# Retention and a maxout FFN on one core: key scaling moved from GpSimd to ScalarE, and the order of retention's VectorE steps changed

## The chip, the cores and the metric

One core of a Trainium2 chip runs the whole program. The metric is the device time of one execution in microseconds (us). Five runs of the kernel before took 780.17 to 783.39 us, median 781.77. All data is fp32.

## The reference, cut to what matters

```python
# B, H, S, D = 8, 8, 576, 64;  4608 tokens, d_model 512 = H*D, d_ff 768
scores = q @ k.T / sqrt(D)                       # per batch and head
ret    = scores * gamma[h] ** (i - j)  (0 where j > i)
x      = (ret @ v).transpose(0, 2, 1, 3).reshape(4608, 512)
h      = max(x @ w1, x @ w2, x @ w3)             # 4608 x 768
out    = h @ w_out                               # 4608 x 512
```

The decay gamma^(i-j) is split into a factor for the query's row and one for the key's row. So keys are multiplied by a factor per row and head (the table `gk`, 128 rows x 8 heads), and the result by a query's factor (`gq`). The weights arrive as 64-bit floats and are turned into fp32 on the chip.

## The kernel before, in words

**Two parts that run together.** The tokens are cut into 36 chunks of 128 (`g`), four to a tile of 512 tokens (`t`, 0 to 8). For each tile `ffn(t)` (L681) does the FFN, and while it runs, retention of tile t+1 is done between its matmuls. `ffn` is a generator that stops 12 times a tile; at stop m the main loop (L831) issues what `steps(t + 1)` (L795) has put into slot m. So a slot is a twelfth of a tile.

**The FFN.** The 768 columns are six groups `fb` of 128. Tile 0 multiplies plainly, while VectorE and ScalarE still convert weights (`convert`); tile 1 does groups 2 and 3 plainly, then 0, 1, 4, 5 by products; tiles 2 to 8 do 0, 1, 4, 5, 2, 3, all by products. "By products" is a scheme with fewer multiplications (`up`, L619): 20 block products a group in the order of `PRODUCTS` (L66), each written to PSUM as A, B, C, D or E. A and B share two PSUM buffers, and C, D and E two others. ScalarE copies each finished A and B to SBUF (L633); VectorE adds and compares them in 14 joins a group (L628), which also read C, D and E from PSUM and so free their buffers. Then `downs` (L467) multiplies by `w_out` in seven products with the tags `dx`, `dy`, `dz`; sums of h (L465) and sums of its outputs are made by VectorE and GpSimd.

**Retention of a chunk, from tile 1 on.** Its keys (`kraw`, 128x512) and values are loaded by SP's DMAs; `load` is itself put into the queue `urgent`. `decay(g)` (L230) scales the keys in place on GpSimd, in one instruction (L236). `transposes(g)` (L244) makes transposed keys and queries: on TensorE with copies on ScalarE for chunks 4 to 6, by two VectorE transposes from chunk 7 on. `chunk_scores(g)` (L287) does the matmuls of scores and state (`sk`, L294 and L298), and then four VectorE steps: two masks (`mask`, L302), which turn `sk` into masked scores `m`, and two `keep_chunk` steps (L310), which carry the state `va` on; after the second one GpSimd multiplies the state by `gs_of` (L312). `values(a, b)` (L354) does the output matmuls `o` (L378) of a pair of chunks, and `output` the multiplication by `gq` and, at a tile's end, 13 sums of x (`X_SUMS`).

**What sets VectorE's order.** The order on each engine is that in which the program issues. From tile 1 on, retention's VectorE steps don't go out at once: `soon` (L177) appends them to the queue `urgent`. During a group of products, `ffn` lets one out after every odd step and every fifth step, 12 of 20. `scores()` and `values()` begin by letting out all that is still there (`chore(len(urgent))`). So the four steps of a pair's first chunk all go out as soon as the second chunk's `scores` starts; those of the second chunk go out one by one. Sums of weights stand in a second queue, `chores`.

**Slots of a pair (a, b), before.** m: transposes(b), decay(b). m+2: scores(a), scores(b), load of b+2. m+3: decay(a+2). m+4: values(a, b), transposes(a+2), load of a+4. Here m is 0 for a tile's first pair and 6 for its second. Chunks 4 to 7, during tile 0, have an order of their own.

**Buffers.** Raw keys have three buffers, raw queries and transposable keys two, state `va` four, PSUM tiles for retention four (`ps_r`).

**The start.** Chunks 0 to 3 are done before `ffn(0)`, in the order written at L751 to L793: loads, decay, transposes, scores, state and values of each. `key_masks` (L343, GpSimd) makes the mask table `gm`; `carry` (L337, ScalarE) copies the last state and the factors `gs_of`.

Of the kernel before, what the change touches and what calls it, by code (L numbers as in the profile page):

```python
# [45 lines left out]
ALU = mybir.AluOpType  # L46
# [34 lines left out]
def kernel(  # L81
# [14 lines left out]
    nc = tc.nc  # L96
    P = 128
    B, H, S, D = q.shape
# [6 lines left out]
    CPT = NT // C  # L105
# [21 lines left out]
    gk = const.tile([C, H], FP32, name="gk")  # L127
# [24 lines left out]
    raws, vds, vas, qks, ms, sts, states, kvs = {}, {}, {}, {}, {}, {}, {}, {}  # L152
# [10 lines left out]
    def half(j):  # L163
        return slice(D * j, D * (j + 1))

    def place(g, c):

        return (g * C + D * c) % S // D

    late, chores, urgent, spread = {}, deque(), deque(), []  # L170

    def chore(n=1):
        for _ in range(n):
            if urgent or chores:
                (urgent or chores).popleft()()
# [54 lines left out]
    def decay(g):  # L230
        factor = gk[:].unsqueeze(2).to_broadcast([C, H, D])
        if g < CPT:
            t = vds[g] = vpool.tile([C, H, D], FP32, tag="va1", name="vd")
            nc.gpsimd.tensor_tensor(t[:], raws.pop(("v", g))[:], factor, op=ALU.mult)
            return
        nc.gpsimd.tensor_tensor(raws["k", g][:], raws["k", g][:], factor, op=ALU.mult)  # L236
        for c in range(2):
            if place(g, c) == 0:
                nc.gpsimd.memset(vas[g, c][half(1 - c)], 0.0)
# [28 lines left out]

    def scores(g):
        chore(len(urgent))  # L270
        if g >= CPT:
            chunk_scores(g)
            return
        qT, kT = qks[g]["q"], qks[g]["k"]
        s = [ps_r.tile([C, NP, C], FP32, tag="r", name=f"s{j}") for j in range(2)]
        for p in range(NP):
            for j in range(2):
                r = half(j)
                nc.tensor.matmul(s[j][:, p, :], lhsT=kT[r, p, :], rhs=qT[r, p, :], start=True, stop=True)
        for j in range(2):  # L280
            t = sts[g, j] = att.tile([C, NP, C], FP32, tag=f"m{j}", name="st", bufs=3)
            nc.vector.tensor_tensor(t[:], s[j][:], causal[:].unsqueeze(1).to_broadcast([C, NP, C]), op=ALU.mult)
# [54 lines left out]
    def carry():  # L337

        for j in range(2):
            nc.scalar.copy(vas[CPT, 0][half(1), j::2, :], states[CPT][half(j)])  # L340
            nc.scalar.copy(gs_of[half(1), j::2].unsqueeze(2), gs[half(j), :, 0:1])

    def key_masks():  # L343
        for c in range(2):
            nc.gpsimd.tensor_tensor(gm[half(c)], causal[half(c), half(c)].unsqueeze(1).to_broadcast([D, H, D]),
                                    gk[half(c)].unsqueeze(2).to_broadcast([D, H, D]), op=ALU.mult)
# [252 lines left out]
    def weight_sums(fp):  # L599

        def step(dst, a, sign, b):
            combine(*(factor(n, slice(2 * fp, 2 * fp + 2)) for n in (dst, a, b)), sign)

        for dst, _, a, sign, b in W_SUMS:
            chores.append(partial(step, dst, a, sign, b))
        chores.append(partial(summed_fp.add, fp))

    def late_room():
        pool = late["pool"]
        late["W"] = [pool.tile([P, NF, P], FP32, name=f"n{n}") for n in range(1, 9)]  # L610
        late["X"] = {n: pool.tile([P, NH], FP32, name=n)[:] for n in sorted({x[0] for x in X_SUMS})}
# [3 lines left out]
    def convert(n):  # L615
        for _ in range(n):
            next(converting, None)
# [60 lines left out]
    def ffn(t):  # L678

        h = hpool.tile([P, NF, NT], FP32, tag="h", name="h")  # L680
        if t == 0:  # L681
            for fp, i in units:
                for fb in (2 * fp, 2 * fp + 1):
                    maximum = up_plain(t, h, fb, i)
                    if CPT not in qks:
                        maximum()
                        transposes(CPT)
                        decay(CPT)
                        convert(4)
                        continue  # L690
                    convert(4)
                    maximum()
                yield
            convert(6)
            for fb, _ in enumerate(downs_plain(t, h)):
                convert(4 if fb < 2 else 4 * len(pieces))
                if fb == 2:
                    while_converting.close()
                    late["pool"] = ctx.enter_context(tc.tile_pool(name="late", bufs=1))
                    late_room()  # L700
                    sums_of_outs()
                elif fb > 2:
                    chore({3: 4, 4: 0, 5: 2}[fb])
                if fb in (1, 3):
                    yield
            yield
            return
        if t == 1:
            spread.append(True)
            weight_sums(0)  # L710
            weight_sums(2)
        plain = (2, 3) if t == 1 else ()
        order = (2, 3, 0, 1, 4, 5) if t == 1 else (0, 1, 4, 5, 2, 3)
        total = sum(24 if fb in plain else len(PRODUCTS) for fb in order)
        count = parts = 0
        for n, fb in enumerate(order):
            if fb not in plain:
                while fb // 2 not in summed_fp:
                    chore()
            steps_of_one = up_plain_all(t, h, fb) if fb in plain else up(t, h, fb)  # L720
            for step, cost in enumerate(steps_of_one):
                if fb in plain:
                    chore(4 if (fb, step) == (plain[-1], 1) else 8)
                elif step % 2 or step % 5 == 4:
                    chore(len(urgent) > 0)
                elif step % 4 == 2 and chores:
                    chores.popleft()()
                count += cost or 1
                if count * (NF // 2 * 3) >= (parts + 1) * total:
                    parts += 1  # L730
                    yield
            if n % 2:
                sums_of_hidden(h, fb // 2)
                if fb in plain:
                    weight_sums(fb // 2)
        chore(len(urgent))
        for n, _ in enumerate(downs(t, h)):
            chore(4)
            if n in (1, 3):
                yield  # L740
        yield
# [13 lines left out]
    load_weights(1)  # L755
    load(CPT)
    decay(0)
    transposes(0)
    for c in range(2):
        of_rows = out_decay[:, NP // 2 * c:NP // 2 * (c + 1), :].rearrange("(b p) u c -> p b (u c)", b=2)  # L760
# [8 lines left out]
    scores(1)  # L769
    first_output()  # L770
    transposes(2)
    decay(2)
    load_values(CPT)
    load_weights(4)
    state(1)
    keep(1)
    values(1)
    transposes(3)
    decay(3)
    scores(2)  # L780
    scores(3)
    state(2)
    keep(2)
# [4 lines left out]
    convert(4)  # L788
    state(3)
    keep(3)  # L790
    key_masks()
    carry()
    convert(2)  # L793

    def steps(t):  # L795


        todo = [[] for _ in range(3 * CPT)]

        def at(n, *what):  # L800
            for step, *args in what:
                args = [g for g in args if g < NG] if step is values else args
                if args and args[0] < NG:
                    todo[n].append(partial(soon, partial(step, *args)) if step is load else partial(step, *args))

        if t == 1:
            a, b, c, d = range(CPT, 2 * CPT)
            at(0, (load, b))
            at(1, (scores, a))
            at(2, (transposes, b), (decay, b), (load, c))  # L810
            at(3, (scores, b), (load_blocks, d, 0))
            at(4, (load_blocks, d, 1, 2))
            at(5, (values, a, b), (load_blocks, d, 3), (load, d))
            at(6, (transposes, c), (decay, c), (load_blocks, d + 1, 0))
            at(7, (transposes, d), (decay, d), (load_blocks, d + 1, 1, 2))
            at(8, (scores, c), (scores, d), (load_blocks, d + 1, 3), (load, d + 1))
            at(9, (load_blocks, d + 2, 0, 1))
            at(10, (decay, d + 1), (load_blocks, d + 2, 2))
            at(11, (values, c, d), (load_blocks, d + 2, 3), (load, d + 2), (transposes, d + 1))
            return todo  # L820
        for n in range(0, CPT, 2):
            a, b, m = CPT * t + n, CPT * t + n + 1, 6 * (n // 2)
            at(m, (transposes, b), (decay, b))
            if a == 2 * CPT:
                at(m, (load, a + 2))
            at(m + 2, (scores, a), (scores, b), (load, b + 2))
            at(m + 3, (decay, a + 2))
            at(m + 4, (values, a, b), (transposes, a + 2), (load, a + 4))
        return todo

    for t in range(N // NT):  # L831
# [56 lines left out]
```

## Time and profile before

| | before |
|---|---|
| five runs | 781.13, 781.77, 783.39, 781.93, 780.17 us, median 781.77 |
| the profiled execution's own time | 781.13 us |
| its span in the profile | 779.4 us |
| mean granted TensorE clock | 0.991 |
| GpSimd, key scaling, 128x512 (L236) | 32 instructions, 1.13 us each |
| GpSimd, state times `gs_of` (L312) | 28 instructions, 1.177 us each |
| ScalarE, copies of A and B (L633) | 276 and 230 instructions, 0.372 us each |
| VectorE, mask of half a chunk (L302) | 64 instructions, 0.688 us each |
| DMA, mean | 76 GB/s |

How to read it: the span runs from the first to the last instruction, and the execution's own time is 1.7 us longer. Busy times are of one engine each and overlap. PE is TensorE's matmuls, PEld its weight loads, DVE is VectorE, ACT ScalarE, POOL GpSimd, SP the engine that issues DMAs. In a line of the timeline the first two numbers are start and length, a name `out<-in` gives the buffers, a shape partitions x elements, xN counts instructions drawn together, and a bracket names the wait in front and what ended it. Engines run their own queues in order, so an instruction that waits holds up all behind it on that engine.

### The profile page before, as it was taken

The page shows a single profiled execution, that of the slowest core. Times are in us where ns is not written, and L with a number is a line of the kernel's source. Part 1 is how long each engine was busy: PE and PEld are TensorE (multiplying, and loading weights), DVE is VectorE, ACT ScalarE, POOL GpSimd, SP SyncE. Part 2 cuts the span into 40 slices and gives each one's busy share as a digit, 9 for nine tenths or more (in the row PEclk, how much of TensorE's full clock was granted, in tenths as well). Part 3 has the DMA queues.
Part 4 walks back from the last instruction along what each step waited for, and adds up shares of the span by engine and source line. Part 5 has one row for each costly group of instructions (what it writes and reads, how often), then busy time and mean ns, then how long its engine had stood idle before and what let it go on. Part 6 is the DMA issues. An engine that isn't in the chain of part 4 may idle for free.

```text
span 779.4 us, 16192 instructions
## 1 busy us (share of the span) xinstructions
PE 751.0 (96%) x6040; PEld 607.5 (78%) x6040; DVE 615.1 (79%) x1270; ACT 353.6 (45%) x869; POOL 125.0 (16%) x138
## 2 busy tenths in 40 slices
PE   8799989999899999999989999999989998999998
PEld 7544444488788888888878887888878887888887
DVE  2889999799979876988598959886889678865672
ACT  3676642155145524462345435451546064524651
POOL 2310113031203030203030302110122003010000
PEclk9989999999999999999999999999999999999999
DMA  9986751424042413342243325141515141001001
GB/s 226 229 203 144 200 116 55 84 52 84 14 105 45 78 46 83 68 77 47 68 83 56 58 66 95 29 82 59 90 28 98 40 88 37 1 15 41 1 1 54
DMA packets 230110, 59.40 MB, mean 76 GB/s; under 512 B 210960, under 2 KB 228752, under 8 KB 230032
## 3 DMA queue, kind: packets, MB, share of 16 engines
q1 hardware_dynamic: 229456, 58.04, 34.4%
q8 instruction: 47, 0.77, 0.4%
q10 hardware_dynamic: 576, 0.33, 0.2%
q14 instruction: 31, 0.25, 0.1%
HBM read 48.89 MB, written 9.44 MB: 75 GB/s over the span
## 4 chain that ended last, share of the span: by engine, by line
PE 74%; DVE 17%; ACT 3%; issue 2%; DMA 2%; SPq 1%; POOL 0%; DVEq 0%; ACTq 0%
PE a L648 15%; PE b L648 13%; PE dx L488 10%; PE c L648 7%; PE dz L488 5%; DVE part L628 5%; PE e L648 5%; PE d L648 4%; PE o L378 4%; PE down L658 3%; DVE m L302 3%; PE up L671 3%; DVE va L310 2%; PE dy L488 2%; PE sk L294 2%
## 5 line engine op out<-in xcount | busy, mean ns | idle before, releaser
L628 DVE TENSOR_TENSOR part<-part 128x256 f32<-128x256 f32 x460 | 221.9, 492 | 64.1 <-ACT part L633 56.2
L633 ACT COPY part<-a 128x256 f32<-128x256 f32 x276 | 102.8, 372 | 73.3 <-PE a L648 60.4
L633 ACT COPY part<-b 128x256 f32<-128x256 f32 x230 | 85.7, 372 | 101.7 <-PE b L648 93.0
L671 PE MATMUL up<-xT,w 128*128 128x512 f32 (+2 forms) x200 | 87.0, 590 | 3.2 <-DVE w L577 3.2
L312 POOL TENSOR_TENSOR va<-va,gs_of 64x512 f32<-64x512 f32 x28 | 33.0, 1177 | 325.9 <-DVE va L310 165.7
L648 PE MATMUL a<-s,w 128*128 128x256 f32 x276 | 82.7, 381 | 0.7 <-ACT part L633 0.7
L648 PE MATMUL b<-s,n 128*128 128x256 f32 x276 | 82.2, 379 | 0.2 <-ACT part L633 0.2
L671 PEld LDWEIGHTS up<-xT,w 128*128 128x128 f32 x200 | 37.5, 194 | 46.6 <-issue 39.7
L648 PE MATMUL d<-s,w 128*128 128x256 f32 x184 | 55.6, 384 | 8.4 <-DVE part L628 8.4
L648 PEld LDWEIGHTS a<-s,w 128*128 128x128 f32 x276 | 51.9, 190 | 9.2 <-ACT part L633 1.9
L648 PEld LDWEIGHTS b<-s,n 128*128 128x128 f32 x276 | 52.4, 190 | 7.7 <-ACT part L633 0.7
L648 PE MATMUL c<-xT,w 128*128 128x256 f32 x184 | 56.0, 386 | 0.0
L648 PE MATMUL b<-xT,n 128*128 128x256 f32 x184 | 55.3, 382 | 0.0
L302 DVE TENSOR_TENSOR m<-sk,gm 64x512 f32<-64x512 f32 x64 | 44.1, 688 | 5.1 <-PE sk L298 4.0
L628 DVE TENSOR_TENSOR h<-part 128x256 f32<-128x256 f32 x92 | 42.7, 464 | 6.9
L648 PE MATMUL e<-xT,w 128*128 128x256 f32 x184 | 47.2, 379 | 0.0
L648 PE MATMUL a<-xT,n 128*128 128x256 f32 x184 | 47.2, 379 | 0.0
L648 PEld LDWEIGHTS d<-s,w 128*128 128x128 f32 x184 | 34.7, 191 | 14.6 <-DVE part L628 10.0
L488 PE MATMUL dx<-To,H 128*128 128x256 f32 (+1 forms) x204 | 44.9, 370 | 0.0
L495 ACT COPY part<-dx 128x256 f32<-128x256 f32 (+1 forms) x34 | 10.5, 362 | 74.1 <-PE dx L488 74.1
L465 POOL TENSOR_TENSOR H<-h,H 128x256 f32<-128x256 f32 x24 | 19.2, 801 | 152.5 <-DVE H L464 128.9
L633 ACT COPY part<-d 128x256 f32<-128x256 f32 x92 | 34.3, 372 | 15.3 <-PE d L648 10.2
(119 smaller groups left out, 1383.6 us busy)
## 6 DMA issues: line engine op xcount, KB each, us to landing
bits<-in_moe_w_dram SPq DMA_DIRECT2D x36, 256.0 KB, 4.6
out_dram<-osb SPq DMA_DIRECT2D x35, 256.0 KB, 2.1
kraw<-in_k_dram SPq DMA_DIRECT2D x32, 256.0 KB, 3.0
va<-in_v_dram SPq DMA_DIRECT2D x64, 128.0 KB, 3.2
qraw<-in_q_dram SPq DMA_DIRECT2D x232, 32.0 KB, 2.2
kxraw<-in_k_dram SPq DMA_DIRECT2D x232, 32.0 KB, 2.1
bits<-in_moe_w_out_dram SPq DMA_DIRECT2D x6, 512.0 KB, 3.9
qraw<-in_q_dram SPq DMA_DIRECT2D x6, 256.0 KB, 4.3
```

Of the source, the lines that this page charges most:

```text
L294: nc.tensor.matmul(sk[c][half(c), h, :], lhsT=kr[half(c), h, :], rhs=vas[g, c][half(c), h, :], start=True, stop=True)
L302: nc.vector.tensor_tensor(ms[g, c][half(c)], sk[1 - c][half(c)], gm[half(c)], op=ALU.mult)
L310: nc.vector.tensor_tensor(to[half(c)], sk[c][half(c)], vas[g, c][half(1 - c)], op=ALU.add)
L312: nc.gpsimd.tensor_tensor(to[half(1)], to[half(1)], gs_of[half(1)].unsqueeze(2).to_broadcast([D, H, D]), op=ALU.mult)
L378: nc.tensor.matmul(o[0][half(c), n % 2, n // 2, half(m)], lhsT=vas[g, m][:, h, :], rhs=ms[g, m][:, h, :], start=m == 0 and n == 0, stop=Tr ...
L465: urgent.append(lambda: (pool(s3, a11, a21, op=ALU.subtract), pool(s4, a12, s2, op=ALU.subtract)))
L488: nc.tensor.matmul(o, lhsT=hS[n](fp)[:, m * P:(m + 1) * P], rhs=late["T"][n][:, fp, cols], start=first and fp == 0 and (m == 0 or last and ...
L628: nc.vector.tensor_tensor(out, a, b, op=op)
L633: nc.scalar.copy(t[:], ps[step[0]][:])
L648: nc.tensor.matmul(ps[chain][:], lhsT=factor(w, fb), rhs=xS[t][x], start=n == 1, stop=ends, skip_group_check=True)
L658: nc.tensor.matmul(b[:], lhsT=h[:, fb, m * P:(m + 1) * P], rhs=w_sb["out", fb], start=(fb == 0), stop=(fb == NF - 1))
L671: nc.tensor.matmul(ps[:, cols], lhsT=w_sb[i, fb][:, dc * P:(dc + 1) * P], rhs=xT[t][:, dc, cols], start=dc == 0 and cols.start == 0, stop= ...
```

## The change

1. **Keys to ScalarE.** From tile 1 on, `decay` no longer issues one GpSimd multiplication of 128x512 but puts eight ScalarE multiplications of 128x64 (one head each, with the head's column of `gk` as a factor per partition) into a new queue, `scaling`. One goes out at every third step of a group of products (`step % 3 == 2`), two after each product of `downs`, and what is left at the start of `scores`. It concerns chunks 10 to 35: GpSimd has 26 fewer instructions and ScalarE 208 more.
2. **A thinner queue.** `urgent` is let out after steps with `step % 4 == 1`, five of 20, and after other odd steps only if more than six are waiting. Tile 1 keeps the rate of before.
3. **One slot earlier.** Scores of a pair go out at m+1 instead of m+2, the scaling of a+2 at m+2, that of b+2 at m+3 (it was at the start of the next pair, m+6). Values stay at m+4. The first pair of tile 2 is the exception: its scores stay at m+2, its values go to m+5.
4. **The first chunks.** `key_masks` goes from behind all chunks to just after `decay(0)`. `carry` goes into `ffn(0)`, after `decay(4)`, and its two copies of `gs_of` become `state_factors`, after `transposes(2)`. `scores(2)` goes ahead of `transposes(3)`.

Instructions per engine: TensorE and SP have the same ones in the same number, VectorE the same ones in another order.

```diff
+    late, chores, urgent, scaling, spread = {}, deque(), deque(), deque(), []
+
+    def scale(n=1):
+        for _ in range(min(n, len(scaling))):
+            scaling.popleft()()
...
-        nc.gpsimd.tensor_tensor(raws["k", g][:], raws["k", g][:], factor, op=ALU.mult)
+        kr = raws["k", g]
+        if spread:
+            scaling.extend(partial(nc.scalar.mul, kr[:, h, :], kr[:, h, :], gk[:, h:h + 1]) for h in range(H))
+        else:
+            nc.gpsimd.tensor_tensor(kr[:], kr[:], factor, op=ALU.mult)
...
     def scores(g):
         chore(len(urgent))
+        scale(len(scaling))
...
-            nc.scalar.copy(gs_of[half(1), j::2].unsqueeze(2), gs[half(j), :, 0:1])
+    def state_factors():
+        for j in range(2):
             nc.scalar.copy(gs_of[half(1), j::2].unsqueeze(2), gs[half(j), :, 0:1])
...
                         decay(CPT)
+                        carry()
...
-                elif step % 2 or step % 5 == 4:
+                elif step % 2 and (step % 4 == 1 or t == 1 or len(urgent) > 6) or t == 1 and step % 5 == 4:
                     chore(len(urgent) > 0)
...
+                if step % 3 == 2:
+                    scale()
...
             chore(4)
+            scale(2)
...
     decay(0)
+    key_masks()
     transposes(0)
...
     transposes(2)
+    state_factors()
     decay(2)
...
     values(1)
+    scores(2)
     transposes(3)
     decay(3)
-    scores(2)
     scores(3)
...
-    key_masks()
-    carry()
...
-            at(m, (transposes, b), (decay, b))
-            if a == 2 * CPT:
-                at(m, (load, a + 2))
-            at(m + 2, (scores, a), (scores, b), (load, b + 2))
-            at(m + 3, (decay, a + 2))
-            at(m + 4, (values, a, b), (transposes, a + 2), (load, a + 4))
+            first_pair = a == 2 * CPT
+            s = m + 2 if first_pair else m + 1
+            at(m, (transposes, b))
+            if first_pair:
+                at(m, (decay, b), (load, a + 2))
+            at(s, (scores, a), (scores, b), (load, b + 2))
+            at(s + 1, (decay, a + 2))
+            at(s + 2, (decay, b + 2))
+            at(s + 3, (values, a, b), (transposes, a + 2), (load, a + 4))
```

## The prediction

> **What bounds the kernel now.** I read the page first, then who waited for whom, then the stretch of time around the longest wait on each engine. From the page:
>
> ```profile
> PE 751.0 (96%) x6040; PEld 607.5 (78%) x6040; DVE 615.1 (79%) x1270; ACT 353.6 (45%) x869; POOL 125.0 (16%) x138
> ...
> PE   8799989999899999999989999999989998999998
> DVE  2889999799979876988598959886889678865672
> ...
> PEclk9989999999999999999999999999999999999999
> ```
>
> TensorE is busy nearly always, so a gain can come only from places where it stands still or its clock is low. Work per tile is fixed: 20 products a group, each two records 0.216 apart (0.432 us). Starts of TensorE records that came later than this pace add up to little, and the view of waits names their cause:
>
> ```profile
> PE d L648 <- DVE part L628: 8.4, 4, 2.3
> PE dy L488 <- DVE h L628: 3.8, 3, 2.4
> ...
> PE sk L298 <- ACT m L263: 2.4, 1, 2.4
> ```
>
> (Columns: total us, times, longest.) The four waits of `d` lie at 406, 487, 569 and 651 us, once a tile in tiles 4 to 7. Here is the first one on TensorE, VectorE and GpSimd (start, length):
>
> ```profile
> 403.34 0.59 PE L648 MATMUL a<-s,n 128*128 128x256 f32 x2
> 406.22 0.70 PE L648 MATMUL d<-s,w 128*128 128x256 f32 x2 [2.29 <-DVE part L628]
> ```
>
> ```profile
> 391.61 1.39 DVE L302 TENSOR_TENSOR m<-sk,gm 64x512 f32<-64x512 f32 x2 [0.34 <-PE sk L298]
> 393.01 1.41 DVE L310 TENSOR_TENSOR va<-sk,va 64x512 f32<-64x512 f32 x2
> 394.46 0.68 DVE L302 TENSOR_TENSOR m<-sk,gm 64x512 f32<-64x512 f32 x1
> 395.07 1.00 DVE L628 TENSOR_TENSOR part<-part 128x256 f32<-128x256 f32 x1
> ...
> 399.18 2.79 DVE L628 TENSOR_TENSOR part<-part 128x256 f32<-128x256 f32 x3
> 402.01 1.12 DVE L628 TENSOR_TENSOR h<-part 128x256 f32<-128x256 f32 x1
> ...
> 405.74 0.42 DVE L628 TENSOR_TENSOR part<-e,part 128x256 f32<-128x256 f32 x1
> ```
>
> ```profile
> 399.29 1.22 POOL L312 TENSOR_TENSOR va<-va,gs_of 64x512 f32<-64x512 f32 x1 [3.50 <-PE e L648]
> 400.59 1.10 POOL L236 TENSOR_TENSOR kraw<-kraw,gk 128x512 f32<-128x512 f32 x1
> ...
> 402.12 0.72 POOL L465 TENSOR_TENSOR H<-h 128x256 f32<-128x256 f32 x1
> ```
>
> Product 13 (`d`) takes the PSUM buffer of `e`, so it needs the join of E and B1 (`part<-e,part`). That join stands in VectorE's queue behind eight retention steps (masks L302, keeps L310, 0.69 each) and 13 joins. VectorE has no gap from 391.61 to 406.16: 14.55 us. TensorE, meanwhile, wants 12.2: of the scores' 2.1 us (390.33 to 392.44) 0.8 is left at 391.61, then products 7 to 19 and 0 to 12, 26 x 0.432 = 11.2, and 0.2 of small gaps. The difference, 2.35, is the stall (2.45 over the pace). Second reading: a join of two SBUF tiles takes 422 ns alone (376 of the 460 `part<-part`), and 807 on average when a GpSimd step overlaps it. In the 14.55 us this adds 0.58 + (2.79 - 1.35) + 0.70 = 2.7 us, of which one L236 is about 0.72 (1147 against 422).
>
> Over the pace, tiles 2 to 7 lose 1.59, 0.87, 2.45, 2.73, 2.56 and 3.95 us: 14.15 in all. The last has 1.1 us of half clock behind its stall (64 `o` records take 3.10 instead of 2.02). Tile 1 loses 2.59 at 201.67 (`dy` waits for h). Tile 8, which has no retention to do, loses nothing.
>
> **The change, part by part.**
>
> *Keys to ScalarE.* GpSimd loses 26 of its 32 L236 (1.13 each; chunks 10 to 35), ScalarE gains 26 x 8 = 208 pieces of 128x64. No row shows such a piece. ScalarE bounds: a 64x4 copy out of SBUF takes 0.19, and the nearest form with a per-partition operand is
>
> ```profile
> L561 ACT ACTIVATE expo<-expo,inf 128x512 int32<-128x512 f32 x24 | 17.3, 722 | 0.8
> ```
>
> Copies of 256 and 512 columns (372, 579 ns) give 0.81 ns a column, so 722 - 448 x 0.81 = 0.36 us; I take it, by this row's form. 208 x 0.36 = 75 us on an engine with 426 us free. What counts is the queue: a piece stands between the copy of a B and of an A, and TensorE's next A waits for the latter. The cover:
>
> ```profile
> 382.67 0.37 ACT L633 COPY part<-b 128x256 f32<-128x256 f32 x1 [0.49 <-PE b L648]
> ...
> 383.33 0.59 PE L648 MATMUL b<-s,n 128*128 128x256 f32 x2
> ```
>
> The copy ends at 383.04, 0.29 before the next `b`; TensorE resumes 0.06 after its releaser (406.16 to 406.22), so a copy may be 0.23 late. Queued ScalarE steps start 0.09 before the former ends (two L290 of 0.61 take 1.14). A copy, then the piece, then the A copy: 0.28 + 0.27 = 0.55 after the B copy's start instead of 0.43: 0.12 late, hidden. From 0.47 us a piece on, the cover is gone. At 0.72 each of some 91 pieces (136 lie in the products, four of six at such a spot) costs 0.25: 22 us. The first piece also waits for its keys' DMA, with all copies behind it: the keys of chunk a+2 are issued at 388.45 and 389.09 and land 3 us later, 392.1; the copy before the piece is at 393.6, so 1.5 us is spare. SP's order is unchanged; later transposes delay its later transfers by some 4 us, and those keys then have 3 us left.
>
> The Trainium skill speaks against this: "VectorE: DVE Perf Modes", The TRN2 errata, says that each SBUF-source instruction of VectorE and ScalarE pays its fixed latency anew, and advises tiles of 512 elements or more; "ScalarE: Activation LUTs", What ACT_TABLE_LOAD costs, would make a piece 186 + 93 + 53 = 0.33 us by estimate, so eight cost 2.7 us for one 1.13. The trace makes both harmless while ScalarE idles over half the time; by that price the copy is 0.09 late instead of 0.12.
>
> *Retention's steps spread, scores one place (1/12 tile) earlier.* The four steps of chunk a still go at once, those of b at every fourth product. Counted in the new order, from the first mask to the end of the next E join VectorE has 6 retention steps (4.15), 10 joins (4.25) and one L312 overlap (0.58): 9.0 us. TensorE has 0.8 + 6 + 13 products (8.2) + 0.2 = 9.2. So the stall goes; for 0.5 us of error either way I keep 0 to 0.5 and take 0.2 per half tile. What is late next: the `dy` behind the second half: 9.0 + two keeps, eight joins, one overlap (5.5) = 14.5 against 9.2 + 7 products + `dx` + two `dy` (6.5) = 15.7; it holds by 1.2. Tiles 2 to 7: 14.15 - 12 x 0.2 = 11.7 gained. The GpSimd part alone would leave 2.35 - 0.72 = 1.6 a tile.
>
> *Tile 1* keeps its faster rate; its eight steps move from the fourth group before the third one's end. By its rows they start at 183.66, and 8 x 0.69 + 11 joins (4.7) + a weight sum (0.4) + 0.72 end the next E join at 195.0. TensorE would have been there at 180.6 + 2.2 + 8 x 0.432 + 5.6 = 191.9: a new stall of 3.1. Then 7 products, `dx` and two `dy` lead to 201.5, where it is 201.67 now: no gain, bounds -1 to +1.
>
> *First chunks.* Today ScalarE waits 2.7 us for the state (30.97) before `carry`, and the copies of the first chunks stand behind that; `sk` starts at 37.31, 3.4 us after `up` ended, and the clock then stands at 0.52 until 43.7. After: the carry comes last, the mask tables (2.4 us of GpSimd) leave the place where they stretch three conversions by 0.84, and 31.0 is when the h copy starts; eight copies (3.0) bring `sk` to about 35.0. But up to 108 us VectorE's weight conversion sets the end (TensorE waits for w at 66 and w_out at 108), so only VectorE's lead counts: the conversion that waits for `mant` at 38.34 gets it at 31.4 + 0.6 + 3.0 + 0.75 (carry) + 0.75 = 36.5: 1.8 gained. Bounds 0 (given back at a DMA) and 4 (the clock dip after 108.4 goes too). Scores(2) ahead of the transposes: 0.3, inside this.
>
> **Sum:** 11.7 + 1.8 + 0 = 13.5; 781.13 (profiled execution; span 779.4) less 13.5 is 767.6. The median of the runs, 781.77, lies 0.64 above: **768**.
>
> **Rivals.** *The burst stays too long* (chance 0.20): if a spread step costs VectorE more or a GpSimd overlap falls on one more join (0.72), the stall returns at the E join in both halves: 0.2 + 0.7 each, 12 x 0.7 = 8.4 less: 776. For it: the margin is 0.2 us. Against: L236 leaves just this stretch. *No measurable change* (0.05): the edit only moves stalls, as in tile 1. *ScalarE's queue becomes the bound* (0.13): slower from about 0.61 us a piece on (91 x 0.14 = 13), with 0.72: 781.1 - 13.5 + 22 = 790. For it: the only ScalarE rows with a pointer operand are 0.72 to 0.76. Against: those have eight times the columns. Forecast itself (within 763 to 772): 0.62.
>
> What a measurement can tell from no change is about 0.2% (1.6 us). Faster 0.62 + 0.20 = 0.82, same 0.05, slower 0.13. The range 763 to 777 holds forecast and first rival, with the tile 1 and head bounds in it.
>
> **What would show it.** Right: `d` and `dy` waits for VectorE at 406 to 651 gone or under 0.5, tile period near 78.5 instead of 81.6; a new `d` wait of about 3 in tile 1; `sk` near 35; pieces of 0.3 to 0.4 us; no `a` wait for ScalarE. Wrong: `PE a` waiting for ScalarE often; pieces over 0.47; a ScalarE wait for `kraw`'s DMA; the E join still late in tiles 4 to 7.

## The result, and the profile after

The changed kernel takes 779.83 us (median of 32 runs, 775.83 to 781.54) where the kernel before takes 781.77: a ratio of 0.9969, 95% interval 0.9960 to 0.9978. It is faster, by 0.3% where 1.8% were forecast. The profiled execution took 778.52 us (before: 781.13).

First the page of the changed kernel: busy time, then the slices and the clock.

```profile
PE 752.0 (97%) x6040; PEld 603.7 (78%) x6040; DVE 595.8 (77%) x1270; ACT 396.7 (51%) x1077; POOL 93.4 (12%) x112
...
PE   8898989998999999999999999999999999999998
...
PEclk9999999999899999999999999999999999999999
...
L174 ACT ACTIVATE kraw<-kraw,gk 128x64 f32<-128x64 f32 x208 | 66.9, 349 | 0.3
```

GpSimd lost 32 us, VectorE 19 without losing an instruction, and a key piece takes 0.349 us. TensorE's busy time *rose* by 1.0 at equal work, and one slice near 200 us has a lower clock. The last row holds the key pieces; ScalarE waited only 0.3 us in front of all 208 of them.

Who waited for whom on TensorE in tiles 2 to 7 (220 to 704 us; total us, times, longest; a third row, 0.5 us of `sk`, is left out):

```profile
PE a L660 <- ACT part L645: 2.9, 4, 1.4
PE d L660 <- DVE part L640: 2.1, 8, 0.6
```

The four `d` waits of up to 2.3 us are gone, as forecast; eight small ones of 0.6 at most are left. What has grown is `a` waiting for ScalarE. In these tiles of the kernel before it was:

```profile
PE a L648 <- ACT part L633: 0.7, 3, 0.3
```

(Lines have shifted: L648, L633 and L628 are now L660, L645 and L640; L302, L308, L310 are L311, L317, L319.)

Where the time went, from the first FFN matmul of one tile to that of the next (for tile 8, to the last matmul), in us:

| | to tile 1 | tile 1 | tiles 2 to 7 | tile 8 |
|---|---|---|---|---|
| before | 132.96 | 84.84 | 488.45 | 70.3 |
| after | 131.10 | 88.93 | 483.62 | 70.3 |
| difference | -1.86 | +4.09 | -4.83 | 0 |
| forecast | -1.8 | 0 | -11.7 | 0 |

So two terms failed. Tile 1 first: TensorE around 190 us.

```profile
189.09 0.59 PE L660 MATMUL b<-s,n 128*128 128x256 f32 x2
189.52 0.66 PE L660 MATMUL a<-s,n 128*128 128x256 f32 x2
193.81 1.22 PE L660 MATMUL d<-s,w 128*128 128x256 f32 x2 [3.63 <-DVE part L640]
194.82 1.06 PE L660 MATMUL b<-xT,n 128*128 128x256 f32 x2
195.68 1.06 PE L660 MATMUL a<-s,w 128*128 128x256 f32 x2
```

The same instructions that took 0.59 take 1.06 after the wait, with starts 0.86 apart instead of 0.43. A table of stretches shows why (length, busy time of each engine, then the granted clock, DMA share, GB/s):

```profile
190.00:192.00 2.00, 0.18 (x1) 0.00 (x0) 1.97 (x3) 0.60 (x3) 1.19 (x1) 1.00 0.39 60
192.00:196.00 4.00, 2.19 (x5) 1.83 (x6) 3.83 (x10) 0.62 (x2) 1.27 (x3) 0.57 0.58 131
196.00:200.00 4.00, 4.00 (x12) 3.19 (x12) 2.32 (x7) 1.48 (x5) 0.00 (x0) 0.57 0.00 0
200.00:204.00 4.00, 4.00 (x20) 3.51 (x19) 3.76 (x10) 1.78 (x7) 0.71 (x1) 1.00 0.00 0
```

From 192.6 to 199.4 us the clock was halved. The wait cost 3.8 us over the pace and the slow matmuls after it 2.8.

The second term: the longest `a` wait in tiles 2 to 7, on VectorE, ScalarE and TensorE.

```profile
515.40 0.69 DVE L311 TENSOR_TENSOR m<-sk,gm 64x512 f32<-64x512 f32 x1
...
516.12 0.58 ACT L317 COPY va<-sk 64x512 f32<-64x512 f32 x1 [1.40 <-DVE m L311]
516.61 0.36 ACT L645 COPY part<-a 128x256 f32<-128x256 f32 x1
...
517.02 0.70 PE L660 MATMUL a<-s,w 128*128 128x256 f32 x2 [1.41 <-ACT part L645]
```

This is no key piece. Where a sequence begins inside a chunk (seven times in the run), `keep_chunk` copies the new state on ScalarE, and that copy starts as VectorE's second mask ends, a mask that the thin queue has put late (run 9 tests this). ScalarE works in order, so the copy of `a` stands behind it and TensorE behind that.

### The profile page after: what moved, and what is told of

The parts are those of the page before. It is cut to its first block, busy times and chain, and to the rows that moved or that the text cites. A ratio compares the mean times of both kernels' runs of the same rounds, so it can differ in the third digit from the quotient of the medians.

```text
span 776.8 us, 16355 instructions
## 1 busy us (share of the span) xinstructions
PE 752.0 (97%) x6040; PEld 603.7 (78%) x6040; DVE 595.8 (77%) x1270; ACT 396.7 (51%) x1077; POOL 93.4 (12%) x112
## 4 chain that ended last, share of the span: by engine, by line
PE 77%; DVE 14%; DMA 3%; SPq 2%; issue 2%; ACT 1%; DVEq 0%
PE a L660 15%; PE b L660 13%; PE dx L500 11%; PE c L660 6%; PE dz L500 5%; PE d L660 5%; PE up L683 5%; PE e L660 4%; PE o L390 4%; DVE part L640 4%; DVE m L311 3%; PE down L670 3%; PE dy L500 3%; PE sk L303 2%; DVE va L319 2%
## 5 line engine op out<-in xcount | busy, mean ns | idle before, releaser
L640 DVE TENSOR_TENSOR part<-part 128x256 f32<-128x256 f32 x460 | 208.8, 463 | 68.4 <-ACT part L645 60.2
L645 ACT COPY part<-a 128x256 f32<-128x256 f32 x276 | 101.9, 369 | 64.4 <-PE a L660 58.5
L645 ACT COPY part<-b 128x256 f32<-128x256 f32 x230 | 85.7, 373 | 86.2 <-PE b L660 79.9
L683 PE MATMUL up<-xT,w 128*128 128x512 f32 (+2 forms) x200 | 85.1, 580 | 5.3 <-DVE w L589 5.3
L660 PE MATMUL a<-s,w 128*128 128x256 f32 x276 | 82.9, 382 | 2.5 <-ACT part L645 2.5
L660 PE MATMUL b<-s,n 128*128 128x256 f32 x276 | 82.1, 379 | 0.0
L321 POOL TENSOR_TENSOR va<-va,gs_of 64x512 f32<-64x512 f32 x28 | 31.0, 1108 | 307.4 <-DVE va L319 194.1
L174 ACT ACTIVATE kraw<-kraw,gk 128x64 f32<-128x64 f32 x208 | 66.9, 349 | 0.3
L660 PE MATMUL d<-s,w 128*128 128x256 f32 x184 | 57.2, 393 | 5.8 <-DVE part L640 5.8
L660 PEld LDWEIGHTS a<-s,w 128*128 128x128 f32 x276 | 51.4, 190 | 12.0 <-ACT part L645 3.9
L660 PEld LDWEIGHTS b<-s,n 128*128 128x128 f32 x276 | 52.4, 190 | 7.1
L660 PE MATMUL b<-xT,n 128*128 128x256 f32 x184 | 57.5, 395 | 0.0
L660 PE MATMUL c<-xT,w 128*128 128x256 f32 x184 | 54.7, 379 | 0.0
L311 DVE TENSOR_TENSOR m<-sk,gm 64x512 f32<-64x512 f32 x64 | 44.0, 688 | 8.5 <-PE sk L307 7.2
L660 PE MATMUL a<-xT,n 128*128 128x256 f32 x184 | 47.9, 383 | 0.4 <-ACT part L645 0.4
L660 PE MATMUL e<-xT,w 128*128 128x256 f32 x184 | 47.2, 379 | 0.0
L640 DVE TENSOR_TENSOR h<-part 128x256 f32<-128x256 f32 x92 | 40.6, 441 | 7.2 <-DVE part L640 0.5
L660 PEld LDWEIGHTS d<-s,w 128*128 128x128 f32 x184 | 34.2, 192 | 15.4 <-DVE part L640 11.1
L645 ACT COPY part<-d 128x256 f32<-128x256 f32 x92 | 34.3, 373 | 14.5 <-PE d L660 10.5
```

Of the source, the lines that this page charges most:

```text
L174: scaling.popleft()()
L311: nc.vector.tensor_tensor(ms[g, c][half(c)], sk[1 - c][half(c)], gm[half(c)], op=ALU.mult)
L321: nc.gpsimd.tensor_tensor(to[half(1)], to[half(1)], gs_of[half(1)].unsqueeze(2).to_broadcast([D, H, D]), op=ALU.mult)
L640: nc.vector.tensor_tensor(out, a, b, op=op)
L645: nc.scalar.copy(t[:], ps[step[0]][:])
L660: nc.tensor.matmul(ps[chain][:], lhsT=factor(w, fb), rhs=xS[t][x], start=n == 1, stop=ends, skip_group_check=True)
```

## The experiments

Theory A, from the traces: the key pieces cost nothing and taking GpSimd away from VectorE is what gains; the new order loses it again in tile 1 (eight steps in front of an E join) and at the state copies. Rival B: the pieces hold up ScalarE, and the order is what gains. Tile times are of the profiled execution, ratios are against the kernel before on the same chip.

**1. Keys alone.** The kernel before with the queue `scaling`; the only slots changed are those of `decay`:

```diff
-            at(m, (transposes, b), (decay, b))
+            at(m, (transposes, b))
...
-            at(m + 4, (values, a, b), (transposes, a + 2), (load, a + 4))
+            at(m + 4, (decay, b + 2), (values, a, b), (transposes, a + 2), (load, a + 4))
```

> The kernel before, with the keys scaled by ScalarE in pieces (and the scaling of chunk b+2 begun two slots earlier, as the change has it), but with retention's steps, the scores and the first chunks in their old places. Theory A (the pieces are free, a GpSimd step in the burst of VectorE steps costs it 0.72 us): the d waits of tiles 4 to 7 go from 2.4 to about 1.6 us, tile 1's dy wait loses 0.7, in all 4 to 5 us: 777. Theory B (the pieces hold up ScalarE's copies, and that ate what the order gained): 782 or more, with waits of TensorE's a for ScalarE of 4 us or more.

Measured: 775.91 us, ratio 0.9913 (0.9885 to 0.9940): this part alone beats the whole change. Tiles 2 to 7 take 482.43. TensorE's waits there:

```profile
PE d L657 <- DVE part L637: 5.1, 4, 1.3
PE a L657 <- ACT part L642: 0.7, 3, 0.4
PE dy L497 <- DVE h L637: 0.5, 1, 0.5
```

The four `d` waits went from 2.1 to 1.3 each, and `a` hardly waits. Theory A holds, rival B falls.

**2. All but the keys.** The changed kernel with `if False:` for `if spread:` in `decay`, so that GpSimd scales every key, at the slots of the change.

> The changed kernel, but every key scaled by GpSimd in one instruction at the slot where the change queues its pieces. Theory A: the E joins of the new order are already 0.2 to 0.8 us late, so each GpSimd step that falls on the stretch before them costs up to 0.72: 4 to 8 us slower than the changed kernel, 784 to 788. Theory B (pieces on ScalarE cost the 3.6 us in which a waits for ScalarE): 776.

788.43 us, ratio 1.0064 (1.0041 to 1.0086): the new order without the key part is slower than the kernel before. Tiles 2 to 7 take 488.07, as before the change, and tile 1 89.46. So the order gained nothing by itself (the GpSimd scaling stands at new slots here; it was not run at the old ones with the new order). And with no key piece on ScalarE, `a` waits for it in tiles 2 to 7 as it did in the changed kernel:

```profile
PE a L660 <- ACT part L645: 3.5, 4, 2.1
```

**3. Tile 1 at the old slots.**

```diff
-            s = m + 2 if first_pair else m + 1
+            s = m + 2 if t == 2 else m + 1
...
-            at(s + 3, (values, a, b), (transposes, a + 2), (load, a + 4))
+            at(m + 4, (values, a, b), (transposes, a + 2), (load, a + 4))
```

> The changed kernel, but the scores and values of tile 2's two pairs (which are done during tile 1) at the slots of before (m+2 and m+4). Theory A (the new E join stall of 3.8 us in tile 1 and the half clock that follows it are lost time): tile 1 falls from 88.9 to about 85 us, in all 775 to 776. Theory B (the time is only moved: the old dy wait of 2.6 and a later clock dip come back, or tile 2 begins with more behind it): 779 to 780.

775.98 us, ratio 0.9912 (0.9885 to 0.9939). Tile 1 takes 84.17, with one `dy` wait of 1.7. The loss was lost time, not moved time.

**4. Tile 1 at the new slots, but thin.** Instead of moving tile 1 back, its last two groups get the thin rate:

```diff
-elif step % 2 and (step % 4 == 1 or t == 1 or len(urgent) > 6) or t == 1 and step % 5 == 4:
+elif step % 2 and (step % 4 == 1 or t == 1 and n < 4 or len(urgent) > 6) or t == 1 and n < 4 and step % 5 == 4:
```

> The changed kernel, with only its exception for tile 1 taken away in that tile's last two groups, so that five of 20 steps let a retention step out there. Theory A (the rate alone makes tile 1's stall: six instead of eight steps in front of the E join, and with a shorter stall the clock keeps up): the d wait falls from 3.6 to about 1.6 us, tile 1 from 88.9 to 84.5 to 85.5, in all 775.5 to 777. Theory B (the earlier place makes it whatever the rate): 779 to 780.

777.67 us, ratio 0.9935 (0.9917 to 0.9954). Tile 1 takes 84.70, its `d` wait is 2.2 us, and the clock stays up. So it was tile 1's release rate. In this trace seven steps, not six, stand in front of the join (185.26 to 195.48 us), and with them the early slot costs tile 1 nothing against before.

**5. The first chunks as before.** The four edits of the first chunks (the head) undone.

> The changed kernel, but the first chunks in the order of before. Theory A (the head gave 1.9 us): 781.7, with tile 1 starting at 133.0 instead of 131.1. Theory B (VectorE's conversion sets the end up to there and the head edit gives nothing that lasts): 779.8.

780.55 us, ratio 0.9972 (0.9955 to 0.9990), against 0.9969 for the whole change: theory B, no difference. In its trace `sk` comes at 37.4 instead of 34.5, and TensorE waits for converted weights twice (5.0 us in all) instead of three times (7.0): part of what `sk` gains is waited for there. Tile 1 starts 3.4 us later, behind three dips of the clock instead of one, but is 2.76 shorter: it has the same `d` stall, and no dip of the clock behind it. But see run 15.

**6. The state copy on VectorE.**

```diff
-                nc.scalar.copy(to[half(c)], sk[c][half(c)])
+                nc.vector.tensor_copy(to[half(c)], sk[c][half(c)])
```

> The changed kernel, but where a sequence begins inside a chunk the new state is copied out of PSUM by VectorE instead of ScalarE (seven copies in the run). Theory A (that ScalarE copy waits for a mask that stands late in VectorE's queue, and holds up the copies of A behind it): the four waits of a for ScalarE, 2.9 us on the trace and 3.6 over the pace, go: 776 to 777.5. Theory B (the key pieces make those waits, or the copy's 0.6 us lengthens the stretch before an E join by as much): 779 to 781.

776.80 us, ratio 0.9921 (0.9896 to 0.9946). All of TensorE's waits in tiles 2 to 7:

```profile
PE d L660 <- DVE part L640: 2.1, 9, 0.3
```

The `a` waits of the view are gone to the last one, with all key pieces in place, and tiles 2 to 7 take 479.54, 4.1 less.

**7. The same copy in the old order.** Run 1 with the edit of run 6.

> Keys on ScalarE as in the first experiment (places and order of before), and the state copy at a sequence's start on VectorE. Theory A (with the old places the mask is done before the copy is due, so little waits behind it: 1.7 us of a and b waits in that run): 0.5 to 1.7 us faster than the first experiment, 0.989 to 0.991 of before, and the d waits of 1.4 us in tiles 4 to 7 stay. Theory B (the copy alone is what held both orders back): 4 us faster, 0.986.

776.06 us, ratio 0.9923 (0.9906 to 0.9940): the same as run 1. Tiles 2 to 7 take 481.75, 0.7 less. In the old order the mask comes sooner: in run 1 the copy that waits 1.40 us in the changed kernel waits 0.34 for it.

**8. Two pieces at a time.**

```diff
-                if step % 3 == 2:
-                    scale()
+                if step % 6 == 2:
+                    scale(2)
```

> The changed kernel, but during the products the key pieces go out two at a time at every sixth step instead of one at every third. Theory A (one piece of 0.35 us, or 0.25 in the queue, fits into the 0.29 us that a copy of A has to spare, two don't): some 60 small waits of a for ScalarE of 0.1 to 0.2 us, 783 to 790. Theory B (ScalarE is half idle, the pieces cost nothing in any grouping): 779 to 780.5.

783.28 us, ratio 1.0002 (0.9983 to 1.0021): 0.3% slower than the change, at the low end of theory A. Tiles 2 to 7 take 487.68, 4.1 more. One of the spots, ScalarE and then TensorE:

```profile
436.96 0.37 ACT L645 COPY part<-b 128x256 f32<-128x256 f32 x1 [0.49 <-PE b L660]
437.36 0.59 ACT L174 ACTIVATE kraw<-kraw,gk 128x64 f32<-128x64 f32 x2
437.86 0.35 ACT L645 COPY part<-a 128x256 f32<-128x256 f32 x1
```

```profile
437.63 0.59 PE L660 MATMUL b<-s,n 128*128 128x256 f32 x2
438.26 0.70 PE L660 MATMUL a<-s,n 128*128 128x256 f32 x2
```

The copy of `a` starts 0.90 after that of `b` instead of 0.43, and TensorE's next `a` starts 0.63 after `b` instead of 0.43. In tiles 2 to 7, 72 `a` products start over 0.03 late where 16 did. The copy is 0.47 late and TensorE 0.20, so 0.27 is covered: the cover that the prediction worked out (0.23) is real and about that small.

**9. The old rate with the new slots.** `elif step % 2 or step % 5 == 4:` in all tiles.

> The changed kernel, but the queue of VectorE steps is let out at the rate of before (12 of 20 steps) in all tiles. Theory A (with the scores one slot earlier an E join comes only nine products later, and only the thin rate keeps the second chunk's steps behind it): two to three more steps of 0.69 us lie before each E join, d waits of 1.5 to 2 us in both halves of a tile, 12 to 18 us slower than the changed kernel: 792 to 798. Theory B (the rate matters little, the place of the burst sets the wait): within 4 us, 776 to 784.

780.96 us, ratio 0.9969 (0.9950 to 0.9988), just that of the change. Theory A was wrong here, and this row shows how:

```profile
PE d L660 <- DVE part L640: 5.7, 9, 1.1
PE sk L307 <- issue: 0.7, 1, 0.7
PE a L660 <- ACT part L645: 0.4, 1, 0.4
```

The `d` waits grow by 3.6 us, less than I put them at; the `a` waits shrink by 2.5, since the masks come sooner (the state copy that waited 1.40 us for one waits 0.42). What the thin queue saved at the E joins it gave back at the copies.

**10. The pieces put together.** Run 3, the copy of run 6, and a queue that skips the step just in front of the E join:

```diff
-elif step % 2 and (step % 4 == 1 or t == 1 or len(urgent) > 6)
+elif step % 2 and (step in (5, 9, 13, 17) or t == 1 or len(urgent) > 6)
```

> The changed kernel with tile 2's chunks at their old slots, the state copy on VectorE, and the queue let out after steps 5, 9, 13 and 17 only (from tile 2 on), so that the second mask of chunk b stands behind the E join instead of in front. Theory A (what is left in tiles 2 to 7 is 0.4 us of lateness per E join and the a waits): from 776.0 less 3.5 less about 3: 769 to 771, with the d waits of about 0.4 gone. Theory B (the mask only moves to another join that is as tight): 774 to 777.

768.11 us, ratio 0.9809 (0.9779 to 0.9838). Tiles 2 to 7 take 475.10, 13.4 less than before. The skip was not run alone; run 6, which has the rest in these tiles, took 479.54, so it is worth about 4.4. The second chunk's second mask, which stood in front of the E join in the changed kernel, now stands behind it. VectorE in the changed kernel and, in the second view, in this run:

```profile
388.27 1.41 DVE L311 TENSOR_TENSOR m<-sk,gm 64x512 f32<-64x512 f32 x2 [0.78 <-PE sk L307]
...
394.58 0.68 DVE L311 TENSOR_TENSOR m<-sk,gm 64x512 f32<-64x512 f32 x1
...
396.62 0.69 DVE L311 TENSOR_TENSOR m<-sk,gm 64x512 f32<-64x512 f32 x1
397.34 0.42 DVE L640 TENSOR_TENSOR part<-e,part 128x256 f32<-128x256 f32 x1
```

```profile
390.57 0.68 DVE L311 TENSOR_TENSOR m<-sk,gm 64x512 f32<-64x512 f32 x1
...
392.50 0.42 DVE L640 TENSOR_TENSOR part<-e,part 128x256 f32<-128x256 f32 x1
392.95 0.69 DVE L311 TENSOR_TENSOR m<-sk,gm 64x512 f32<-64x512 f32 x1
```

**11. Run 10 with the keys on GpSimd.**

> The fastest version so far with every key scaled by GpSimd in one instruction again. Theory A (each of them stretches VectorE's joins by 0.7 us wherever VectorE is late; the good order has 0.2 us of lateness in one half of a tile, none in the other): 12 halves of 0.3 to 0.7 us, 4 to 8 us slower, 772 to 776, still faster than before. Theory B (the order was all of the gain): 768 to 769.

775.54 us, ratio 0.9925 (0.9902 to 0.9948). Tiles 2 to 7 take 482.50, 7.4 more. So this order with its state copy on VectorE gains 0.7% without the key part too, which the change's order did not (run 2). The waits, from tile 1 on, are back:

```profile
PE dy L500 <- DVE h L640: 4.3, 4, 2.4
PE d L660 <- DVE part L640: 2.6, 6, 0.7
```

**12. and 13. Tile 1 again.** Run 10 with tile 2's second pair early (m+1) and the thin rate of run 4, and with it later still (scores at m+3, values at m+5).

> The fastest version so far with tile 2's second pair at the changed kernel's early slots, but the thin release in tile 1's last two groups as well. Theory A (tile 1's new stall is the number of retention steps in front of the last group's E join, 8 there): now 5 to 6 stand in front, the stall falls from 3.8 to 1.5 to 2.5 us, dy doesn't wait, and the clock may still dip: tile 1 at 84 to 87 us, in all 768 to 771. Theory B (the stall comes from the weight sums and the tile's own load): 3.5 us or more again, with the clock dip, 772.

> The fastest version so far with tile 2's second pair still later: scores after tile 1's last product, values at the tile's end. Theory A (tile 1's dy wait of 1.85 us is the retention steps in front of the last joins): the wait goes, tile 1 at 82.3 us, in all 766. Theory B (the eight steps then stand in front of the sums of h or the sums of x, and TensorE waits there): 768 to 770, with a wait of dx, o or a new b at the tile's end.

Early: 767.54 us, ratio 0.9813 (0.9796 to 0.9829), and tile 1 at 83.57. Its one wait from 133 to 764 us:

```profile
PE d L660 <- DVE part L640: 1.0, 1, 1.0
```

Late: 773.90 us, ratio 0.9891 (0.9875 to 0.9908). Tile 1 takes 84.08, but tile 2 83.4 instead of 79.0:

```profile
PE a L660 <- ACT part L645: 2.3, 1, 2.3
PE dx L500 <- DVE H L476: 1.6, 1, 1.6
PE sk L307 <- DVE m L179: 1.2, 1, 1.2
```

Theory B: `dx` waits because the steps stand in front of the sums of h, and the next chunk's transposes are late. The longest wait, of `a`, comes of these late transposes too: SP waits 6.3 us for a transpose before it loads new blocks into that buffer, issues the next keys behind them, at 234.40, and the first piece of these keys holds up ScalarE:

```profile
237.42 0.35 ACT L174 ACTIVATE kraw<-kraw,gk 128x64 f32<-128x64 f32 x1 [2.57 <-DMA kraw<-in_k_dram]
237.68 0.35 ACT L645 COPY part<-a 128x256 f32<-128x256 f32 x1
```

```profile
238.08 0.70 PE L660 MATMUL a<-s,n 128*128 128x256 f32 x2 [2.34 <-ACT part L645]
```

The prediction named this danger; of the fourteen traces with pieces it came true in this one alone.

**14. and 15. The head once more.** Run 12 again, and run 12 with the head edits undone, on one chip. Theory A here is that the gain is waited for, theory B that it is 1.8 us.

> The fastest version again, as the partner of the next run on the same chip: 767 to 769.

> The fastest version with the first chunks in the order of before. Theory A (VectorE's weight conversion is busy from 28 us on and sets TensorE's waits for w at 64 us, so whatever the head gains is waited for there): within 0.6 us of its partner. Theory B (the head gives 1.8 us): 1.4 to 2.4 us slower than its partner.

767.48 us, ratio 0.9798 (0.9777 to 0.9819), and 769.31, ratio 0.9832 (0.9812 to 0.9852). Four runs each, 765.22 to 767.57 and 769.12 to 770.62, don't overlap. Here the head gives 1.8 us, so theory B holds, against run 5. In the two traces tile 1 starts at 134.09 and 135.58. What the head is worth is between nothing (run 5) and 1.8 us (run 15), and it stays open. The start of tile 1 in a single trace can't settle it: it lies at 131.10 to 135.79 us in the twelve traces with the new head (mean 133.9) and at 132.96 to 135.59 in the five with the old one (134.3). One effect shows in all: the five have a stretch of half clock between 35 and 44 us, and the twelve have none from 28 to 60 us.

## Why the prediction was wrong

**The keys: right.** A piece takes 0.349 us (0.36 said), one is hidden and two are not. The wait for the keys' DMA, which was priced at nothing with 1.5 to 3 us to spare, came only in run 13. Without GpSimd's step the `d` wait is 1.42 over the pace (1.6 said). What the prediction did not see is that this part alone gives 6.0 us in tiles 2 to 7, more than the whole change there.

**The first chunks: not settled.** 1.8 was said. That the two profiled executions differ by 1.86 is luck, since tile 1 starts anywhere within 4.7 us in traces with the same head; the paired runs give 0 to 1.8. `sk` is at 34.5 (35.0 said), but at 34.5 to 37.2 in the twelve traces, against 36.5 to 37.6 with the old head.

**Tile 1: this step failed.** The new stall was forecast (3.1 us; it is 3.8), and also that `dy` then doesn't wait. The step "no gain, bounds -1 to +1" took TensorE to run at full clock after the stall. The clock was halved for 6.8 us, which cost 2.8, although the prediction's own reading of tile 7 has half clock behind a stall. The dip is in part chance: the same stall drew none in the trace of run 5 (see the last section). Without it the term stays near its bound: run 5, with the same stall and no dip, has tile 1 at 86.17, 1.3 over before. With the stall gone (run 3) or shorter (run 4) the loss is gone.

**Steps spread: this step failed most.** 11.7 us were said for tiles 2 to 7, 4.83 came. The sum left 2.4 for E joins that come 0.2 late. Ten of them are 0.18 to 0.76 late, 3.8 in all: 1.4 of the miss. In the place shown at run 10 (388.27 to 397.76 us) VectorE needs 9.5 us from the first mask to the end of the E join where 9.0 was said, with the six retention steps and ten joins of the count; TensorE would have been there after 9.1 (9.2 said). Another part was not in the sum at all: 3.6 us over the pace in four `a` waits, all at state copies on ScalarE (run 6). The prediction weighed what the *pieces* do to ScalarE's queue, and took the spread steps to be VectorE's alone, though `keep_chunk` has a ScalarE branch that its own code shows. Spreading masks makes them later, and that copy waits for one. Another 0.7 is a wait of `sk` in tile 5; some 1.2 us, in gaps of 0.1 or less, stays open. (The sign "tile period near 78.5" doesn't follow from the sum: 488.45 less 11.7, over six tiles, is 79.5.)

**The rivals.** "The burst stays too long" expected the stall at E joins in both halves; it is there in small. "ScalarE's queue becomes the bound" named the right engine and the wrong instruction. Neither counted a clock that falls after a stall. "No measurable change" came nearest to the number, but its reason, that stalls only move, fails: tile 1's loss was real (run 3), and so was the gain of the keys (run 1).

The forecast sum itself was not out of reach: with the copy on VectorE, the mask behind the E join and tile 1 thinned (run 12) tiles 2 to 7 give 13.4, tile 1 1.3, and the time is 767.5, where 768 was said for the change.

## What to carry to other kernels

When steps are spread to keep one engine's queue short, list who waits for the *last* of them: here a copy on ScalarE, in front of the copies that pace TensorE. Test the parts of a change one by one even if the whole is faster: here one part gave 0.9% and the others took two thirds of it back. And reckon with it that a TensorE stall of two us or more can cost more than its length.

## What the runs showed of the hardware

**A stall can cost twice.** The times at half clock last 3.4 us or twice that, read from the granted clock in slices of 1 us. Cutting the time of twelve traces (the two kernels, runs 1, 2, 4 to 6, 8 to 11 and 14) into steps of 3.41 us in line with those dips, and adding up TensorE's idle time in each step, a rule shows: after 26 us, all 24 steps at full clock with 2.01 us idle or more were followed by half clock, and of the 58 with 1.0 to 1.99 us only one was (1.84). The other five traces, which the rule was not read from, agree: all 12 steps with 2.19 us or more were, and none of 16 with 1.0 to 1.96. So the same 3.6 us wait in tile 1 drew a dip in the changed kernel (2.40 us of it fell into one step) and none in run 5 (1.89 and 1.73); in run 8 a wait of 3.2 drew none (1.36 and 1.89). In the kernel before, stalls of 2.2 to 2.5 us lay in tiles 4 to 7, and only the last drew one (2.06 in one step, against 1.33, 1.71 and 1.85). This is read from traces; no run moved a stall on purpose.

The Trainium skill, "TensorE: Matmul & The Clock Gate", Part 1: The HAM clock gate, says that the clock halves after at least one idle window of about 3.4 us, and that the windows run freely and don't start anew with the kernel. The traces agree with the free-running windows (within a trace the dips lie whole steps apart, and the steps lie differently against the kernel's start from trace to trace); they show that a window need not be idle throughout, some 2.0 of 3.41 us is enough.

The spread between runs goes with it: 16 executions of the changed kernel at a mean clock of 0.991 took 780.4 us on average, three at 0.998 took 776.1.

**VectorE slows beside GpSimd.** The same 1270 VectorE instructions take 19.3 us less in the changed kernel, which has 26 GpSimd steps of 1.13 us fewer. Part of that is the order. With VectorE's order the same, taking the 26 steps away saves 12.6 us (before and run 1), 15.7 (run 2 and the changed kernel) or 17.2 (runs 11 and 10): 0.48 to 0.66 for each.
